# Second unit's rows ahead of weight words, weight words later, and own outputs in a bank of their own, in an mLSTM cell followed by a multiplicative FFN

## The chip, the cores and the metric

The kernel runs on one core of one Trainium2 chip. The metric is device time in microseconds (us), the median of several executions. A core has five engines with a queue each, and the text calls them as the profile does: PE is TensorE (PEld its weight loads), DVE is VectorE, ACT is ScalarE, POOL is GpSimd, SP is SyncE, which here only issues DMAs.

## The reference

```python
B, H, S, D = 4, 8, 768, 40                   # float32 throughout
for t in range(S):                           # mLSTM cell, per batch and head
    m_new  = maximum(f_gate[t] + m, i_gate[t])
    f_stab = exp(f_gate[t] + m - m_new);  i_stab = exp(i_gate[t] - m_new);  m = m_new
    C = f_stab * C + i_stab * outer(v[t], k[t])
    n = f_stab * n + i_stab * k[t]
    y[t] = sigmoid(o_gate[t]) * (C @ q[t]) / maximum(abs(n . q[t]), 1)
x = y as (3072, 320)                         # token rows, heads side by side
out = ((x @ w1) * (x @ w2)) @ w3 @ w_out     # w1, w2: 320 x 1024; w3: 1024 x 1024; w_out: 1024 x 320
```

## The kernel before

**Units and steps.** The recurrence is computed in chunks of 64 tokens; two chunks of one batch (128 tokens, all 8 heads) make a unit. There are 24 units, in order of token block and then batch, so four units are one block of 128 tokens of all batches, and a state is handed on every fourth unit. The main loop (line 727) has 32 steps. Step s loads the rows of unit s + 2 (`load`, `load_o`), computes scores, own weights and state of unit s, the outputs of unit s - 1, transposes k and q of unit s + 1 (`turn`), and makes the decay weights of unit s + 1 (`weights` on ACT, eight exponentials; `masks` on POOL). For the first four units the rows of those weights are spread over the partitions by matmuls (`spread`, tile `ub`), later they come from `UT` by a DVE transpose (`rows_of_u`) or by DMA (`load_u`).

**A unit on PE** (`quarter_work`, line 330) is four groups of small matmuls into the PSUM tiles `cell0` and `cell1`: `ph`, the outputs from the unit's own tokens (`pw` times v); `pi`, the outputs from the state; `ss`, the scores; `pc`, the sums for the state, from the v weighted on POOL (`weighted`, tile `vw`). Each group goes through the four 64 x 64 quarters of the array in turn (`quarters`). A quarter that crosses the halves puts the result of one half of the tokens on the other half of the partitions, so DVE adds `ph` to `h` in four parts (line 400).

**DVE after a unit** (`outputs` and the end of `quarter_work`): `h` from `pi` and the gate (line 395), the four adds, the scores' product (line 373), the state's second part (378 or 380), three passes for the denominator (408, 410, 411), the state's last part (386), then the sigmoid with the denominator and y (416, 418). The state's decay on POOL (line 327) waits for the second part, and the next masks stand behind it on POOL.

**FFN.** x is y transposed (`x_trans` on PE, tile `px`, copied by ACT to `xT`). `up` computes blocks of x w1 and x w2 into PSUM (`pa`, `pb`), `up_rest` adds the last 64 of the 320 rows (weights `wr`), ACT copies the one and DVE multiplies by the other. Up-projections start in step 4 (lists `n_up`, `ups`): steps 4 to 6 use the first half of the 1024 columns, step 7 is the first that uses the second half. w3 and w_out are folded into one matrix (`fold`), so `ffn_out` gives the output directly.

**Weight words.** w1, w2, w3 and w_out are read as 64-bit words and turned into float32 on the chip: `fetch` loads a tile of words by SP, `scale` is two ACT passes (lines 181 and 185; in the opening the second one runs on DVE), `to_f32` is two DVE passes (189 and 190). The tiles are, in order: five for the first half of w1, w2 and their last rows (numbers 0 to 4), five for the second half (5 to 9), eight of w_out, sixteen of w3. `n_cvt[s]` tiles are converted at the end of step s, after the exponentials and `out_gate` in ACT's order, and words are fetched up to a few tiles ahead of the conversions. There are four `raw` buffers and two more in idle memory at the start.

**Order.** PE's order is that of the program. From the opening on, the other engines' orders are held too (`keep_order`), the SP queue among them: a DMA that waits for a buffer holds up all DMAs behind it. `mps` hands out four PSUM banks in rotation to all that isn't `cell`.

Of the kernel before, what the change touches and what calls it, by code (L numbers as in the profile page):

```python
# [8 lines left out]
FP = mybir.dt.float32  # L9
U32 = mybir.dt.uint32  # L10
AF = mybir.ActivationFunctionType
OP = mybir.AluOpType
# [4 lines left out]
def kernel(  # L17
# [26 lines left out]
    nc = tc.nc  # L44
# [3 lines left out]
    P = 128  # L48
# [50 lines left out]
    quarters = ((0, 0), (1, 1), (0, 1), (1, 0))  # L99


    NB, NBQ = 4, 3
    N_DVE = N_U = 10
    q_all = const.tile([P, NBQ * H * DP], FP, name="q_all")
    qbuf = [q_all[:, i * H * DP:(i + 1) * H * DP].rearrange("p (h d) -> p h d", d=DP) for i in range(NBQ)]
    kbuf = [const.tile([P, H, DP], FP, name=f"kbuf{i}") for i in range(NB)]
    vbuf = [const.tile([P, H, D1], FP, name=f"vbuf{i}") for i in range(NB)]
    ident = const.tile([P, P], FP, name="ident")
    state = [[const.tile([P, NP, D1], FP, name=f"state{b}_{i}") for i in range(3)] for b in range(B)]
    aT = const.tile([P, NT2, BH], FP, name="aT")  # L110
    gT = const.tile([P, NT2, BH], FP, name="gT")
    wT = const.tile([P, NT2, BH], FP, name="wT")
    decay = const.tile([P, B * NP, NT], FP, name="decay")
    UT = const.tile([P, 2, NT2, BH], FP, name="UT")
    U_d = dram.tile([NT, BH, L], FP, name="U_d")
    NY = 15
    KC = KF + 1
# [6 lines left out]
        return src[b, :, c * P:(c + 1) * P, :].rearrange("h p d -> p h d")  # L124

    def load(n, which=slice(0, 3)):
        for dst, src in ((kbuf[n % NB][:, :, 0:D], k), (qbuf[n % NBQ][:, :, 0:D], q), (vbuf[n % NB][:, :, 0:D], v))[which]:
            if src is not q or n < N_DVE:
                nc.sync.dma_start(out=dst, in_=rows(src, n))  # L129

# [8 lines left out]
                                      in_=of.rearrange("p (r f) d -> r p (f d)", f=4))  # L139

    def load_o(n):
        o_t[n] = io.tile([P, H, D], FP, name="o_in", tag="o_in", bufs=4)
        nc.sync.dma_start(out=o_t[n], in_=rows(o_gate, n))

    def load_u(n):
# [127 lines left out]
    def cols_of_u():  # L273
        pu = mps([P, 2, GC // 2, GR, BH], "pu")
        for x in range(2):
            for e in range(2):
                for t in range(2):
                    for c in range(GC // 2):
                        t0 = c * P + x * L + t * 32
                        mm(pu[x * L + e * 32:x * L + (e + 1) * 32, t, c].rearrange("p g r -> p (g r)"),  # L280
                           U[:, t0:t0 + 32], ident[0:RG, 0:RG])
        for t in range(2):
            nc.scalar.copy(out=UT[:, t].rearrange("p (g c) r -> p c g r", g=GR), in_=pu[:, t])

    def rows_of_u(n):
        c, b = divmod(n, B)
# [32 lines left out]
    def weighted(n):  # L319
        c, b = divmod(n, B)  # L320
        vw_t[n] = sb.tile([P, H, D1], FP, name="vw", tag="vw")
        nc.gpsimd.tensor_tensor(out=vw_t[n], in0=vbuf[n % NB], op=OP.mult,
                                in1=wT[:, c, b * H:(b + 1) * H].unsqueeze(2).to_broadcast([P, H, D1]))

    def decayed(new, old, n, x):
# [4 lines left out]
    def quarter_work(s, rest):  # L330


        rest()

        def part(j, c0, n):
            return cell[j][:, :, c0:c0 + NP * n].rearrange("p x (n d) -> p x n d", d=n)

        ss, pc, pi = part(0, 0, L), part(0, NP * L, D1), part(1, 0, D1)
        ph = [cell[1][:, x, NP * D1:2 * NP * D1].rearrange("p (h d) -> p h d", d=D1) for x in range(2)]
        n = s - 1  # L340
        if 0 <= n < NU:
            pw, vt, qT = u_t.pop(n), vbuf[n % NB], qT_t.pop(n)
            before = before_t.pop(n)

            for hd in range(H // 2):
                for x, e in quarters:
                    hq = hd if x == e else hd + H // 2
                    mm(ph[x][halves[e], hd, :], pw[halves[x], hq, :], vt[halves[x], hq, :])
            for p in range(NP):
                for hip, x in quarters:  # L350
                    mm(pi[halves[x], hip, p, :], qT[heads[hip], p, halves[x]], before[x][heads[hip], p, :])
        n, first_read = s, None
        if n < NU:
            c, b = divmod(n, B)
            kt, vw = kbuf[n % NB], vw_t.pop(n)
            ends = range(2 if c < NT2 - 1 else 1)
            first, second, after = state[b]
            before_t[n] = first, second
            state[b] = after, second, first
            kT, qT, pw = kT_t.pop(n), qT_t[n], u_t[n]  # L360
            for p in range(NP):
                for hip, x in quarters:
                    mm(ss[halves[x], hip, p, :], kT[heads[hip], p, halves[x]], qT[heads[hip], p, halves[x]])
            for p in range(NP):
                for x, e in quarters:
                    if x in ends:
                        mm(pc[halves[e], x, p, :], kt[halves[x], 2 * p + e, :], vw[halves[x], 2 * p + e, :])
        den = None
        if 0 <= s - 1 < NU:
            den = outputs(s - 1, pi, ph)  # L370
        if n < NU:
            pv = pw.rearrange("p (n two) t -> p two n t", two=2)
            first_read = nc.vector.tensor_tensor(out=pv, in0=ss, in1=pv, op=OP.mult)
        with tc.issue_after(first_read.ins) if first_read else nullcontext():
            if n < NU:

                if c:
                    nc.vector.tensor_tensor(out=second, in0=pc[:, 0], in1=second, op=OP.add)
                else:
                    nc.vector.tensor_copy(out=second, in_=pc[:, 0])  # L380
                if len(ends) > 1:
                    decayed(after, second, n, 1)
            if den:
                done = den()
            if n < NU and len(ends) > 1:
                nc.vector.tensor_tensor(out=after, in0=pc[:, 1], in1=after, op=OP.add)
            if den:
                done = done()
        return done if den else first_read

    def outputs(n, pi, ph):
        c, b = divmod(n, B)
        hs = slice(b * H, (b + 1) * H)
        h = sb.tile([P, H, D1], FP, name="h", tag="h")
        nc.vector.tensor_tensor(out=h.rearrange("p (n two) d -> p two n d", two=2), in0=pi,
                                in1=gT[:, c, hs].rearrange("p (n two) -> p two n", two=2).unsqueeze(3)
                                .to_broadcast([P, 2, NP, D1]), op=OP.mult)
        for x, e in quarters:
            part = h[halves[x], 0:H // 2] if x == e else h[halves[x], H // 2:H]
            nc.vector.tensor_tensor(out=part, in0=ph[x][halves[e]], in1=part, op=OP.add)  # L400

        den = sb.tile([P, H, 1], FP, name="den", tag="den")

        def first():
            V = nc.vector
            V.tensor_scalar(out=den.bitcast(U32), in0=h[:, :, D:D1].bitcast(U32), scalar1=0x7FFFFFFF, scalar2=None,  # L408
                            op0=OP.bitwise_and)
            V.tensor_scalar(out=den, in0=den, scalar1=1.0, scalar2=2.0, op0=OP.max, op1=OP.mult)  # L410
            V.reciprocal(out=den, in_=den)
            return then

        def then():
            e = o_t.pop(n)
            nc.vector.scalar_tensor_tensor(out=e, in0=e, scalar=1.0, in1=den.to_broadcast([P, H, D]), op0=OP.add, op1=OP.mult)
            y_t[n] = sb.tile([P, DM + REM], FP, name="y", tag="y")
            return nc.vector.tensor_tensor(out=y_t[n][:, 0:DM].rearrange("p (h d) -> p h d", d=D), in0=h[:, :, 0:D],
                                           in1=e, op=OP.mult)

        return first

    def send(n):

# [59 lines left out]
    fetch("w12", 0, 0)  # L484
    load(0, slice(2, 3))
    fetch("w12", 1, 0)
    load_o(0)
    fetch("w12", 2, 0)
    idle += [w3o_words[:, i * CW:(i + 1) * CW] for i in range(2)]
    fetch("w12", 3, 0)  # L490
    fetch("w12", 4, 0)
    load(1)
    load_o(1)

    nc.vector.memset(on, 1.0)
    nc.vector.memset(on.rearrange("p (c t) -> p c t", t=L)[:, :, 0:1], 0.0)
# [2 lines left out]
    for i in range(NB):  # L499
        nc.gpsimd.memset(kbuf[i][:, :, D:DP], 0.0)  # L500
        if i < NBQ:
            nc.gpsimd.memset(qbuf[i][:, :, D:DP], 0.0)
        nc.gpsimd.memset(vbuf[i][:, :, D:D1], 1.0)
    for t in state:
        nc.gpsimd.memset(t[0], 0.0)
# [67 lines left out]
    nc.scalar.activation(out=g, in_=U, func=AF.Exp)  # L573
    scale_next(True)
    convert()
    scale_next(True)

    ffn = ctx.enter_context(tc.tile_pool(name="ffn", bufs=2))

# [138 lines left out]
    n_seven = [0] * 19 + [1] * 12 + [0]  # L718
    n_down = [0] * 17 + [2] * 6 + [1] * 7 + [0, 5]
    w12 = [("w12", i, part) for part in range(2) for i in range(2 * KF + 1)]  # L720
    todo = w12[KF * 2 + 1:] + [("wo", i, 0) for i in range(FO)] + [("w3", ko, part) for ko in range(FO) for part in range(2)]
    n_cvt = [2, 1, 1, 1, 2, 2, 3, 3, 3] + [2] * 7
    pinned, ahead = 32, 9
    behind = ExitStack()
    turned, converted, fetched = 0, 2, 2 * KF + 1

    for s in range(len(n_up)):
        if N_U <= s + 3 < NU:
# [84 lines left out]
                scale_next()  # L813
        if N_DVE <= s + 2 < NU:
            load_turned(s + 2)
        while todo and fetched < converted + (2 if s < 2 else 3 if s < ahead - 1 else 4):
            fetch(*todo.pop(0))
            fetched += 1
        if s + 1 == pinned:
# [32 lines left out]
```

## Time and profile before

| | |
|---|---|
| median of 6 runs | 452.76 us (449.69 to 455.21) |
| profiled execution | 452.9 us, span 451.0 |
| PE busy | 428.1 us (95%), 5303 matmul records |
| PE weight loads | 339.8 us (75%) |
| DVE busy | 308.8 us (68%) |
| ACT busy | 150.9 us (33%) |
| POOL busy | 82.0 us (18%) |
| DMA | 51.15 MB, mean 113 GB/s |
| PE busy by stage: 0 to 11, to 22, to 34, to 45, to 56 us | 5.1, 5.1, 12.0, 7.9, 8.6 us |
| PE busy from 150 to 400 us | 250.0 us |

The span is the time from the first to the last instruction; the device time holds 1.9 us more. Busy times overlap between engines. A float32 matmul is two records. Where the page shows a granted clock of 0.5, matmuls take twice as long; before the first change of the clock, at some 39 us, the records show 1.00 whatever the clock was. Of steps 0 to 3 little is dense work; from step 4 on up-projections fill PE.

### The profile page before, as it was taken

What the parts mean: (1) busy time and instruction counts of PE and PEld (TensorE: products, weight loads), DVE (VectorE), ACT (ScalarE), POOL (GpSimd) and SP (SyncE); (2) the same over time, 40 slices, a digit from 0 to 9 for tenths busy, and PEclk for the clock granted to TensorE, in tenths of its full rate; (3) what the DMA queues carried; (4) which work ended last, traced back from release to release, by engine and by line L of the source; (5) the groups of instructions that cost most, each with busy time, mean ns of one, the idle gap of its engine ahead of it and who ended that gap; (6) DMA issues with size and microseconds to landing.
All of it is one profiled execution on the core that took longest, in us unless ns stands there. A gap on an engine that the chain in (4) does not pass through costs nothing.

```text
span 451.0 us, 12926 instructions
## 1 busy us (share of the span) xinstructions
PE 428.1 (95%) x5303; PEld 339.8 (75%) x5303; DVE 308.8 (68%) x645; ACT 150.9 (33%) x409; POOL 82.0 (18%) x154
## 2 busy tenths in 40 slices
PE   4497799999999999999999999999999999999997
PEld 3396687888777888878777878778788777777774
DVE  6347768877958866976695959677698776445800
ACT  4345555666643552453033312203121111001110
POOL 3222534332302202220222203102020000000000
PEclk9998599999999999999999999999999999999999
DMA  8999917679889895779544584663211120000001
GB/s 206 176 181 213 132 32 139 124 161 183 220 175 195 175 189 157 149 160 164 111 86 122 115 158 107 137 122 97 58 32 37 36 49 16 15 16 15 1 30 44
DMA packets 135595, 51.15 MB, mean 113 GB/s; under 512 B 109744, under 2 KB 127344, under 8 KB 135536
## 3 DMA queue, kind: packets, MB, share of 16 engines
q1 hardware_dynamic: 131936, 46.29, 51.7%
q10 hardware_dynamic: 3600, 4.03, 2.6%
q8 instruction: 41, 0.67, 0.6%
q14 instruction: 18, 0.15, 0.1%
HBM read 44.50 MB, written 5.80 MB: 112 GB/s over the span
## 4 chain that ended last, share of the span: by engine, by line
PE 88%; DMA 3%; DVE 2%; SPq 2%; ACT 2%; issue 1%; POOL 1%; POOLq 0%; DVEq 0%; ACTq 0%
PE cell L92 23%; PE pa L92 22%; PE pb L92 14%; PE po L92 13%; PE wp L92 7%; PE p L92 5%; DMA q_all<-in_q_dram 2%; PE pt L95 2%; SPq L174 1%; PE px L95 1%; PE pu L92 1%; PE ub L92 1%; DMA raw<-in_moe_w_dram 1%; DVE h L400 1%; SPq L129 0%
## 5 line engine op out<-in xcount | busy, mean ns | idle before, releaser
L92 PE MATMUL pa<-xT,w 128*128 128x256 f32 x240 | 62.4, 392 | 2.5 <-ACT xT L458 2.5
L92 PE MATMUL po<-w3o,ab 128*128 128x320 f32 x224 | 61.8, 433 | 0.0
L92 PEld LDWEIGHTS po<-w3o,ab 128*128 128x128 f32 x224 | 42.4, 190 | 17.3 <-issue 0.4
L92 PEld LDWEIGHTS pa<-xT,w 128*128 128x128 f32 x240 | 45.6, 195 | 11.0 <-ACT xT L458 3.6
L327 POOL TENSOR_TENSOR state<-state,decay 128x164 f32<-128x164 f32 x40 | 20.4, 511 | 170.4 <-DVE den L408 168.5
L300 POOL TENSOR_SCALAR_AFFINE_SELECT pw<-pw 64x512 f32<-64x512 f32 x48 | 33.7, 703 | 68.6 <-ACT pw L295 67.0
L92 PE MATMUL pb<-xT,w 128*128 128x256 f32 x192 | 46.1, 384 | 0.0
L92 PE MATMUL cell<-w3o,ab 128*128 128x320 f32 x160 | 44.0, 432 | 0.0
L295 ACT ACTIVATE pw<-pw,aT 128x64 f32<-128x64 f32 x160 | 40.3, 339 | 2.8 <-ACT o_sb L706 2.8
L92 PEld LDWEIGHTS pb<-xT,w 128*128 128x128 f32 x192 | 37.2, 194 | 5.3
L604 DVE TENSOR_TENSOR ab<-pb,a_sb 128x512 f32<-128x512 f32 x24 | 16.5, 690 | 34.4 <-ACT a_sb L603 34.4
L92 PEld LDWEIGHTS cell<-w3o,ab 128*128 128x128 f32 x160 | 30.4, 190 | 12.0
L651 DVE SCALAR_TENSOR_TENSOR a_sb<-pa,wo 128x512 f32<-128x512 f32 x12 | 8.3, 692 | 41.8 <-PE pa L92 41.8
L603 ACT ACTIVATE a_sb<-pa 128x512 f32<-128x512 f32 x24 | 14.3, 597 | 67.3 <-PE pb L92 67.3
L92 PE MATMUL pa<-xT,wr 64*64 64x256 f32 x384 | 36.8, 386 | 0.0
L92 PE MATMUL pb<-xT,wr 64*64 64x256 f32 x384 | 36.2, 379 | 0.0
L92 PE MATMUL wp<-wo,w3T 128*128 128x320 f32 x128 | 35.8, 432 | 0.0
L400 DVE TENSOR_TENSOR h<-cell,h 64x164 f32<-64x164 f32 x96 | 31.3, 326 | 1.8
L92 PEld LDWEIGHTS wp<-wo,w3T 128*128 128x128 f32 x128 | 23.7, 190 | 8.9
L92 PEld LDWEIGHTS pa<-xT,wr 64*64 64x64 f32 x384 | 19.0, 132 | 14.8 <-issue 8.9
L706 ACT COPY o_sb<-po 128x320 f32<-128x320 f32 x14 | 6.0, 427 | 67.4 <-PE po L92 67.4
L92 PEld LDWEIGHTS pb<-xT,wr 64*64 64x64 f32 x384 | 20.2, 133 | 3.0
(132 smaller groups left out, 735.4 us busy)
## 6 DMA issues: line engine op xcount, KB each, us to landing
raw<-in_moe_w_dram SPq DMA_DIRECT2D x64, 128.0 KB, 3.3
kbuf<-in_k_dram SPq DMA_DIRECT2D x24, 160.0 KB, 4.5
vbuf<-in_v_dram SPq DMA_DIRECT2D x24, 160.0 KB, 5.1
o_in<-in_o_gate_dram SPq DMA_DIRECT2D x24, 160.0 KB, 4.4
out_dram<-o_sb ACTq DMA_DIRECT2D x24, 160.0 KB, 1.8
raw<-in_moe_w_dram SPq DMA_DIRECT2D x7, 512.0 KB, 5.9
pw<-U_d SPq DMA_DIRECT2D x28, 128.0 KB, 4.0
raw<-in_moe_w_out_dram SPq DMA_DIRECT2D x32, 80.0 KB, 2.1
```

The costliest lines, as they stand in the source:

```text
L92: in_order(nc.tensor.matmul(out, lhsT=lhsT, rhs=rhs, start=start, stop=stop))
L95: in_order(nc.tensor.transpose(out, in_, ident[0:n, 0:n]))
L174: nc.sync.dma_start(out=dst, in_=src)
L295: nc.scalar.activation(out=pw[:, h, :], in_=src[:, h, :], func=AF.Exp, bias=aT[:, c, b * H + h:b * H + h + 1])
L300: nc.gpsimd.affine_select(out=pw[r], in_=pw[r], compare_op=OP.is_ge, fill=0.0, base=0, pattern=[[0, H], [1, L]], channel_multiplier=-1)
L327: nc.gpsimd.tensor_tensor(out=new, in0=old, op=OP.mult, in1=decay[:, b * NP:(b + 1) * NP, 2 * c + x:2 * c + x + 1] .to_broadcast([P, NP, D1]))
L400: nc.vector.tensor_tensor(out=part, in0=ph[x][halves[e]], in1=part, op=OP.add)
L603: nc.scalar.mul(out=a_sb, in_=pa, mul=UP ** -2)
L604: nc.vector.tensor_tensor(out=ab_t[gr][j][:, fs[0]:fs[-1] + 1, t0:t0 + a_sb.shape[-1]], in0=pb, in1=a_sb, op=OP.mult)
L651: nc.vector.scalar_tensor_tensor(out=out, in0=p, scalar=UP ** -2, in1=q, op0=OP.mult, op1=OP.add)
L706: nc.scalar.copy(out=o_sb, in_=po)
```

## The change

Four edits that belong together:

1. **Order of the first loads.** k and q of unit 1 are loaded right behind the second word tile, its v and o next, and the third word tile after them. Tiles 3 and 4 are no longer fetched in the opening. How many tiles are fetched by the end of steps 0 to 7 is now given by a list (`n_fetch`), and conversions (`n_cvt`) come later: by the end of steps 0 to 8 there were 4, 5, 6, 7, 9, 11, 14, 17, 20 tiles converted, now 2, 3, 4, 5, 6, 8, 12, 16, 20. One scaling in the opening is left out with them.
2. **Own outputs of the first five units.** `ph` of units 0 to 4 gets one of the rotating banks, each head's result on its own tokens' partitions, with two quarters of the array in place of four; DVE adds it in one instruction of full size.
3. **The denominator's passes.** The first now stands ahead of the scores' product, the second behind it, the third behind the state's second part.
4. **Buffers.** v and o have five buffers in place of four. `UT` keeps four token blocks in place of six, and its copy is narrower.

```diff
-    NB, NBQ = 4, 3
+    NB, NBQ, NBV = 4, 3, 5
     N_DVE = N_U = 10
+    N_DIAG = 5
...
-    vbuf = [const.tile([P, H, D1], FP, name=f"vbuf{i}") for i in range(NB)]
+    vbuf = [const.tile([P, H, D1], FP, name=f"vbuf{i}") for i in range(NBV)]
...
-    UT = const.tile([P, 2, NT2, BH], FP, name="UT")
+    GC = NT // 3
+    UT = const.tile([P, 2, GC, BH], FP, name="UT")
...
-        o_t[n] = io.tile([P, H, D], FP, name="o_in", tag="o_in", bufs=4)
+        o_t[n] = io.tile([P, H, D], FP, name="o_in", tag="o_in", bufs=5)
...
-            nc.scalar.copy(out=UT[:, t].rearrange("p (g c) r -> p c g r", g=GR), in_=pu[:, t])
+            nc.scalar.copy(out=UT[:, t].rearrange("p (g c) r -> p c g r", g=2), in_=pu[:, t, :, 0:2])
...
-            for hd in range(H // 2):
+            if n < N_DIAG:
+                ph = mps([P, H, D1], "ph")
+                for hq in range(H):
+                    for r in halves:
+                        mm(ph[r, hq, :], pw[r, hq, :], vt[r, hq, :])
+            for hd in range(H // 2 if n >= N_DIAG else 0):
                 for x, e in quarters:
...
             den = outputs(s - 1, pi, ph)
+            den()
         if n < NU:
             pv = pw.rearrange("p (n two) t -> p two n t", two=2)
             first_read = nc.vector.tensor_tensor(out=pv, in0=ss, in1=pv, op=OP.mult)
         with tc.issue_after(first_read.ins) if first_read else nullcontext():
+            if den:
+                den()
...
             if den:
-                done = den()
+                den()
             if n < NU and len(ends) > 1:
                 nc.vector.tensor_tensor(out=after, in0=pc[:, 1], in1=after, op=OP.add)
             if den:
-                done = done()
+                done = den()
...
-        for x, e in quarters:
+        if n < N_DIAG:
+            nc.vector.tensor_tensor(out=h, in0=ph, in1=h, op=OP.add)
+        for x, e in quarters if n >= N_DIAG else ():
...
-        def first():
+        def steps():
             V = nc.vector
-            V.tensor_scalar(...0x7FFFFFFF...)
+            yield V.tensor_scalar(...0x7FFFFFFF...)
-            V.tensor_scalar(out=den, in0=den, scalar1=1.0, scalar2=2.0, op0=OP.max, op1=OP.mult)
-            V.reciprocal(out=den, in_=den)
-            return then
+            yield V.tensor_scalar(out=den, in0=den, scalar1=1.0, scalar2=2.0, op0=OP.max, op1=OP.mult)
+            yield V.reciprocal(out=den, in_=den)
...
     fetch("w12", 1, 0)
+    load(1, slice(0, 2))
     load_o(0)
+    load(1, slice(2, 3))
+    load_o(1)
     fetch("w12", 2, 0)
     idle += [w3o_words[:, i * CW:(i + 1) * CW] for i in range(2)]
-    fetch("w12", 3, 0)
-    fetch("w12", 4, 0)
-    load(1)
-    load_o(1)
...
     scale_next(True)
     convert()
-    scale_next(True)
...
-    todo = w12[KF * 2 + 1:] + [("wo", i, 0) ...
+    todo = w12[3:] + [("wo", i, 0) ...
-    n_cvt = [2, 1, 1, 1, 2, 2, 3, 3, 3] + [2] * 7
+    n_cvt = [0, 1, 1, 1, 1, 2, 4, 4, 4] + [2] * 7
+    n_fetch = [4, 5, 6, 8, 10, 12, 16, 20]
...
-    turned, converted, fetched = 0, 2, 2 * KF + 1
+    turned, converted, fetched = 0, 2, 3
...
-        while todo and fetched < converted + (2 if s < 2 else 3 if s < ahead - 1 else 4):
+        while todo and fetched < (n_fetch[s] if s < len(n_fetch) else converted + 4):
```

More of the change, by code (lines that the diff above doesn't have):

```diff
@@ L126, in load @@
     def load(n, which=slice(0, 3)):
-        for dst, src in ((kbuf[n % NB][:, :, 0:D], k), (qbuf[n % NBQ][:, :, 0:D], q), (vbuf[n % NB][:, :, 0:D], v))[which]:
+        for dst, src in ((kbuf[n % NB][:, :, 0:D], k), (qbuf[n % NBQ][:, :, 0:D], q), (vbuf[n % NBV][:, :, 0:D], v))[which]:
             if src is not q or n < N_DVE:
@@ L321, in weighted @@
         vw_t[n] = sb.tile([P, H, D1], FP, name="vw", tag="vw")
-        nc.gpsimd.tensor_tensor(out=vw_t[n], in0=vbuf[n % NB], op=OP.mult,
+        nc.gpsimd.tensor_tensor(out=vw_t[n], in0=vbuf[n % NBV], op=OP.mult,
                                 in1=wT[:, c, b * H:(b + 1) * H].unsqueeze(2).to_broadcast([P, H, D1]))
@@ L341, in quarter_work @@
         if 0 <= n < NU:
-            pw, vt, qT = u_t.pop(n), vbuf[n % NB], qT_t.pop(n)
+            pw, vt, qT = u_t.pop(n), vbuf[n % NBV], qT_t.pop(n)
             before = before_t.pop(n)
-            for hd in range(H // 2):
+            if n < N_DIAG:
[4 more added lines that the diff above has]
+            for hd in range(H // 2 if n >= N_DIAG else 0):
                 for x, e in quarters:
@@ L404, in outputs @@
         den = sb.tile([P, H, 1], FP, name="den", tag="den")
-        def first():
+        def steps():
             V = nc.vector
-            V.tensor_scalar(out=den.bitcast(U32), in0=h[:, :, D:D1].bitcast(U32), scalar1=0x7FFFFFFF, scalar2=None,
+            yield V.tensor_scalar(out=den.bitcast(U32), in0=h[:, :, D:D1].bitcast(U32), scalar1=0x7FFFFFFF, scalar2=None,
                             op0=OP.bitwise_and)
-            V.tensor_scalar(out=den, in0=den, scalar1=1.0, scalar2=2.0, op0=OP.max, op1=OP.mult)
-            V.reciprocal(out=den, in_=den)
-            return then
-        def then():
+            yield V.tensor_scalar(out=den, in0=den, scalar1=1.0, scalar2=2.0, op0=OP.max, op1=OP.mult)
+            yield V.reciprocal(out=den, in_=den)
             e = o_t.pop(n)
@@ L417, in then @@
             y_t[n] = sb.tile([P, DM + REM], FP, name="y", tag="y")
-            return nc.vector.tensor_tensor(out=y_t[n][:, 0:DM].rearrange("p (h d) -> p h d", d=D), in0=h[:, :, 0:D],
+            yield nc.vector.tensor_tensor(out=y_t[n][:, 0:DM].rearrange("p (h d) -> p h d", d=D), in0=h[:, :, 0:D],
                                            in1=e, op=OP.mult)
-        return first
+        done = steps()
+        return lambda: next(done)
     def send(n):
@@ L502 @@
             nc.gpsimd.memset(qbuf[i][:, :, D:DP], 0.0)
+    for i in range(NBV):
         nc.gpsimd.memset(vbuf[i][:, :, D:D1], 1.0)
@@ L720 @@
     w12 = [("w12", i, part) for part in range(2) for i in range(2 * KF + 1)]
-    todo = w12[KF * 2 + 1:] + [("wo", i, 0) for i in range(FO)] + [("w3", ko, part) for ko in range(FO) for part in range(2)]
-    n_cvt = [2, 1, 1, 1, 2, 2, 3, 3, 3] + [2] * 7
+    todo = w12[3:] + [("wo", i, 0) for i in range(FO)] + [("w3", ko, part) for ko in range(FO) for part in range(2)]
+    n_cvt = [0, 1, 1, 1, 1, 2, 4, 4, 4] + [2] * 7
+    n_fetch = [4, 5, 6, 8, 10, 12, 16, 20]
     pinned, ahead = 32, 9
     behind = ExitStack()
-    turned, converted, fetched = 0, 2, 2 * KF + 1
+    turned, converted, fetched = 0, 2, 3
     for s in range(len(n_up)):
```

## The prediction

> **What bounds the kernel now.** I read the page's strip of 40 slices first, then what TensorE waited for, then its timeline, and last the other engines' timelines around two places.
>
> ```profile
> span 451.0 us, 12926 instructions
> ...
> PE   4497799999999999999999999999999999999997
> ...
> PEclk9998599999999999999999999999999999999999
> ```
>
> From the sixth slice on TensorE is full: 428.1 us busy of 451.0, and of the 22.9 idle only 2.3 lie between 57 us and 400 us (0.84 at 69.9, 0.31 at 106.3, 1.11 at 126.4). So the first 57 us can give something back, and after them every new wait of TensorE is paid in full. Its waits, as total, times and longest:
>
> ```profile
> PE pt L95 <- DMA kbuf<-in_k_dram: 10.3, 2, 5.7
> PE cell L92 <- POOL vw L322: 3.8, 3, 2.6
> PE pa L92 <- ACT xT L458: 2.5, 3, 1.1
> PE pt L95 <- DMA q_all<-in_q_dram: 0.9, 1, 0.9
> ```
>
> The 10.3 us are two waits: 5.7 for the very first rows, which the change leaves, and the second unit's. The timeline shows that one (start, duration, and in brackets the idle time and what ended it), and the first up-projection of two later steps:
>
> ```profile
> 19.32 1.09 PE L95 MATMUL pt<-ident,kbuf 128*128 128x128 f32 x4 [4.60 <-DMA kbuf<-in_k_dram]
> 21.26 1.09 PE L95 MATMUL pt<-ident,q_all 128*128 128x128 f32 x4 [0.85 <-DMA q_all<-in_q_dram]
> ...
> 51.75 3.78 PE L92 MATMUL pa<-xT,w 128*128 128x256 f32 x8 [0.57 <-ACT xT L458]
> ...
> 82.79 1.89 PE L92 MATMUL pa<-xT,w 128*128 128x256 f32 x8
> 84.52 1.67 PE L92 MATMUL pb<-xT,w 128*128 128x256 f32 x7
> ```
>
> The 3.78 at 51.75 against 1.89 for the same eight matmuls is the clock: it was granted at half there.
>
> **Rows of the second unit ahead: -5.6 us at 22 us.** The SyncE queue issues k(1) at 9.85 and q(1) at 10.64, behind five word tiles; they are in use at 19.32 and 21.26. In the new order they follow the second word tile, whose issue ended at 5.22, so they are issued at about 5.3 and 5.7. Issue to landing is 5.7 (k, median of the first 60 us; 9.3 at most) and 6.1 (q; 10.5 at most): landed at 11 to 12, at the very worst 16.2. TensorE's work before them ends at 14.71 and q is wanted 0.9 later. Both waits go. Eight such transposes took 1.95 in step 1 (31.13 to 33.08), so the spreading of step 0 starts at 14.71 + 1.95 = 16.7, not at 22.27: 5.6 earlier. Bounds: 5.0 with the worst landing of q, 5.6.
> What is late next is a chain of computation: from the spreading in step 1 to the up-projection at 51.75 it runs TensorE (spread), ScalarE (eight exponentials, 1.75), GpSimd (two masks 1.38, weighting 0.74 to 0.79), TensorE, transposes, and round again, some 9 us a step. Nothing in the change touches it, so the gain is carried to step 4. The third early scaling that goes from the opening frees ScalarE 0.7 and VectorE 0.43 beside a TensorE that does not wait for them: 0. The narrower copies of line 283 (0.54 for two) save a third at most, behind the exponentials: 0.
> The word tiles that come later are used later too: tile 4 (numbered from 0) is converted at the end of step 3, and by the rows of that step is ready 4.7 us after 51.75 (56.48), wanted 6.2 after it (57.96) at half clock: 0. At full clock it would be wanted 3.5 after: +1.2, but then 2.5 of half clock are saved.
>
> **Five units' own outputs in one bank: +0.9 +0.9 on TensorE.** As many matmuls (32 records a unit), but in two quarters of the array in place of four in turn. Four quarters took 0.43 per unit at full clock (58.81 to 59.24), 0.88 at half (27.54 to 28.42). The nearest row with two column halves is the spreading: 32 in 1.98 (62 ns each) against 0.88 (27 ns) at half clock, so I take double. From below it is 0, if issue and not the array sets the pace. Step 1: +0.9 on the path. Steps 2 and 3: TensorE waits 2.6 and 0.7 for GpSimd's weighting after these, so 0 (at most 0.9 if the slack of step 3 goes). Steps 4 and 5, where TensorE is full: 2 x 0.43 = +0.9. VectorE saves three of four adds (1.34 for four; one of full size like line 395, 0.49): 0.85 a unit, five times. No wait of TensorE is on it, since weighting on GpSimd ends the wait in steps 2 and 3: 0. The extra turn in the four rotating banks is read out in time by the rows of steps 4 and 5: 0. The spreading of step 2 ran at 1.15, as the clock had just risen; 5.6 earlier it may still be slow: +0.4, from 0 to 0.8.
>
> **Denominators' passes spread: 0.** The second pass takes 0.46 on 8 columns where the first takes 0.16: 0.3 is waiting for the first, and goes, per unit. One pass now stands ahead of the scores' product (0.2 later). VectorE idles in the full stage, so neither is paid.
>
> **Five buffers of v and o: 0.** They free the SyncE queue from line 129's wait for TensorE (0.2) and line 143's; no TensorE wait after 22 us names a load of rows.
>
> **Conversions later: +3.4 us in step 7.** Counting the list: before, 11 tiles are converted by the end of step 5; after, 8, and step 6 does tiles 8 to 11. Step 7 is the first that reads the second half of the words, tiles 5 to 9, and tile 8 (w2, second row block) is the second operand of the first pb. It stands in ScalarE's queue behind the exponentials and the gate of step 6, and VectorE waits for ScalarE:
>
> ```profile
> 83.56 2.02 ACT L295 ACTIVATE pw<-pw,aT 128x64 f32<-128x64 f32 x8
> 85.48 0.47 ACT L261 ACTIVATE o_in<-o_in 128x320 f32<-128x320 f32 x1
> ...
> 65.12 0.68 ACT L181 ACTIVATE raw<-raw 128x512 f32<-128x512 f32 x1
> ...
> 65.83 0.77 DVE L189 TENSOR_SCALAR w<-raw 128x512 uint32<-128x512 uint32 x1 [0.18 <-ACT raw L181]
> 66.73 1.00 DVE L190 CUSTOM_DVE_ANT_0 w<-raw,w 128x1024 uint16<-128x1024 uint16 x1
> ```
>
> The scaling can start at 85.84 (where the first of step 6 starts now). A tile of this size took 65.12 to 67.73 = 2.6 from its scaling to its end, so it is ready at 88.4. pb starts at 84.52 and does its first block (two records of 0.22) by 85.0. TensorE stands for 3.4 us. Behind the waiting matmul the whole step is queued: rest, cell, transposes. With GpSimd silent the second pass would end 0.69 (as at 29.36) after the scaling, which takes 1.25 (65.12 to 66.37): ready at 87.8, a wait of 2.8. Tile 9 follows by 1.2 and is wanted 5 later: 0. One wo tile more in each of steps 6 to 8 (0.8 ScalarE, 0.85 to 1.1 VectorE) fits their idle time (2.66 and 1.65 at 88 to 91), except in step 8, where VectorE ends at 116.39 just as its next operand is there: up to 0.9 later into the chain that ends in the 1.11 wait; I take +0.3.
>
> **The clock after that wait: +1.7.** The rows of 2 us (columns: span, busy time and count of TensorE, its weight loads, VectorE, ScalarE, GpSimd, then clock, DMA share, GB/s):
>
> ```profile
> 36.00:38.00 2.00, 0.00 (x0) 0.00 (x0) 0.97 (x2) 1.42 (x3) 1.82 (x3) 1.00 1.32 138
> ...
> 40.00:42.00 2.00, 2.00 (x18) 1.67 (x18) 1.92 (x6) 1.60 (x3) 0.35 (x1) 0.50 0.87 242
> ```
>
> After 2.6 idle (35.7 to 38.3) the clock fell to half for about 3.4 us, though TensorE was busy by then. Idle times of 1.11 and 0.84 did nothing. So 3.4 us of idle should cost half of 3.4 = 1.7; bounds 0 and 5 (below).
> The Trainium skill (TensorE: Matmul & The Clock Gate, section HAM oscillation — how this bites in real kernels) has as its abstract rule that gaps over about 3.4 us are to be avoided. Taken as a threshold, it leaves this one at the edge; with no fall the sum would be 453.2 in place of 454.9. The row at 36 speaks against so high a threshold.
>
> **Sum,** from the profiled execution's 452.9 (451.0 span, 1.9 around it): -5.6 +0.9 +0.4 +0.9 +3.4 +0.3 +1.7 = 454.9. That execution lies 0.1 above the median 452.76, so 454.8 as a median.
>
> **Rivals.**
> *No stall in step 7* (the tile is there after all): 454.9 - 3.4 - 1.7 = 449.8; with a luckier clock in the opening (the half clock at 51.75 cost about 2.7) down to 447. For it: VectorE and ScalarE have idle time in step 6. Against: that time comes before the exponentials' data. 0.15.
> *Stall, clock unmoved*: 453.2; 451 if the opening also warms earlier. 0.23.
> *Slower: the clock stays low after the stall.* From 47 to 57 it was at half for 10 us, since short waits kept coming. If step 7 is followed by the same, the loss is 5.0 and not 1.7: 458.2. It decides if the half clock lasts over 8 us there. Against: what follows the stall is dense. 0.12.
> *The rows do not come earlier* (the queue full, as the third word tile's 2.31 issue hints): the gain is about 2.6, 457.9. 0.03.
>
> **Numbers.** Forecast 454.8 with 0.47, its own range 453.5 to 457.5. Range 449.6 to 458.4: it leaves out the lower half of the first rival and the end of the slow ones. Within 1% is 448.2 to 457.3, about what a measurement of this kernel can tell from no change. Faster by over 1%: a part of the first rival and unseen gains, 0.10. Slower: the two slow rivals and the forecast's tail, 0.23. Same: 0.67.
>
> **What would show it.** No wait before the transposes of unit 1; step 4's first up-projection at 47 to 49 us; own-output matmuls of the first five units at 0.9 us; a TensorE wait of about 3 us on the conversion (line 190) in front of pb near 82 us, and a granted clock of half behind it. The prediction is wrong if the steps 1 to 3 do not keep their 9 us, or if that wait is missing.

## The result and the profile after

The changed kernel takes 454.36 us (median of 37 runs; the kernel before, in its runs beside it, 451.32 of 74): a ratio of 1.0081, 95% interval 1.0063 to 1.0099. The ratio is taken from runs in the faster of two states, so it is not the quotient of the two medians (1.0067). It is 0.8% slower, where 0.45% was forecast. The sum came out close, but two of its terms were far off, in opposite directions.

The page's head and strips of the changed kernel (the profiled execution took 456.5 us):

```profile
span 454.7 us, 12899 instructions
...
PE   4987998899779999999999999999999999999997
...
PEclk9976899999969999999999999999999999999999
```

TensorE is busier than before in slices 2 and 5, but has a new hole in slices 7 and 8 (at about 80 us) and another in slices 11 and 12 (at about 125 us), with a second stretch of reduced clock in slice 12. What TensorE waited for, as total, times, longest:

```profile
PE pa L92 <- ACT xT L468: 7.3, 3, 5.9
PE pt L95 <- DMA kbuf<-in_k_dram: 5.6, 1, 5.6
PE cell L92 <- POOL vw L324: 4.9, 4, 2.2
PE pb L92 <- DVE w L192: 3.5, 1, 3.5
```

The 10.3 us for rows of k are down to 5.6: the second unit's wait is gone. The 3.5 in front of pb is the wait that was forecast; the 5.9 for xT was 1.1 before. TensorE's timeline of the changed kernel at the places the prediction speaks of:

```profile
14.48 1.06 PE L95 MATMUL pt<-ident,kbuf 128*128 128x128 f32 x4
...
16.32 1.98 PE L92 MATMUL ub<-gates,ident 96*64 96x64 f32 x32
18.23 1.93 PE L92 MATMUL pu<-ident,gates 96*32 96x96 f32 x32
...
43.29 3.78 PE L92 MATMUL pa<-xT,w 128*128 128x256 f32 x8 [0.57 <-ACT xT L468]
...
75.52 1.89 PE L92 MATMUL pa<-xT,w 128*128 128x256 f32 x8
77.25 0.59 PE L92 MATMUL pb<-xT,w 128*128 128x256 f32 x2
81.30 1.56 PE L92 MATMUL pb<-xT,w 128*128 128x256 f32 x6 [3.46 <-DVE w L192]
...
128.12 3.78 PE L92 MATMUL pa<-xT,w 128*128 128x256 f32 x8 [5.85 <-ACT xT L468]
```

The same matmuls in the kernel before, where the prediction does not show them:

```profile
22.27 1.98 PE L92 MATMUL ub<-gates,ident 96*64 96x64 f32 x32
24.18 3.43 PE L92 MATMUL pu<-ident,gates 96*32 96x96 f32 x32
...
127.47 1.99 PE L92 MATMUL pa<-xT,w 128*128 128x256 f32 x8 [1.11 <-ACT xT L458]
```

Read as a balance of the two profiled executions (1.6 and 2.2 us above their medians): the spreading of step 0 starts 5.95 us earlier than before (16.32 against 22.27), step 4's first up-projection 8.46 earlier (43.29 against 51.75), step 7 7.27 earlier (75.52 against 82.79). Behind the 3.46 us wait, step 8 has 3.6 left (its up-projection starts at 91.23 against 94.78). At 128.12 the lead is a lag of 0.65 (against 127.47), and the up-projection there runs at half clock, 3.78 for eight matmuls; that makes the lag about 3.7, the difference of the spans.

The first wait is tile 8, as forecast: ScalarE reaches its scaling behind the exponentials, and VectorE ends its second pass at 81.24.

```profile
78.56 0.66 ACT L183 ACTIVATE raw<-raw 128x512 f32<-128x512 f32 x1
...
80.25 0.99 DVE L192 CUSTOM_DVE_ANT_0 w<-raw,w 128x1024 uint16<-128x1024 uint16 x1
```

The second is longer to follow. ScalarE's timeline of the changed kernel shows the copy of xT for unit 7 (line 468) behind the scalings of tiles 20 to 23, each of which waits for its own words:

```profile
119.51 0.69 ACT L183 ACTIVATE raw<-raw 128x512 f32<-128x512 f32 x1 [4.42 <-DMA raw<-in_moe_w_dram]
...
122.10 0.70 ACT L183 ACTIVATE raw<-raw 128x512 f32<-128x512 f32 x1 [1.34 <-DMA raw<-in_moe_w_dram]
...
124.35 0.67 ACT L183 ACTIVATE raw<-raw 128x512 f32<-128x512 f32 x1 [1.00 <-DMA raw<-in_moe_w_dram]
...
126.52 0.65 ACT L183 ACTIVATE raw<-raw 128x512 f32<-128x512 f32 x1 [0.95 <-DMA raw<-in_moe_w_dram]
...
127.61 0.46 ACT L468 COPY xT<-px 128x384 f32<-128x384 f32 x1
```

Why the words are late stands in the SP queue's timeline of the changed kernel. It does nothing from 75.89 on, until at 81.27 the conversion of tile 8 frees a buffer; from there to 122.44 it issues 67 DMAs, 0.61 us each, with hardly a gap, and tiles 20 to 23 are the last sixteen:

```profile
74.86 1.03 SPq L145 DMA_DIRECT2D o_in<-in_o_gate_dram  x1
81.27 8.41 SPq L176 DMA_DIRECT2D raw<-in_moe_w_out_dram  x16
...
113.95 8.49 SPq L176 DMA_DIRECT2D raw<-in_moe_w_dram  x16
```

In the kernel before the last sixteen end at 121.76, 0.7 us earlier than here, though its step 7 begins 7.3 us later:

```profile
113.09 8.67 SPq L174 DMA_DIRECT2D raw<-in_moe_w_dram  x16
```

While the queue stands, the DMA engines stand too (mean busy share 0.00 from 78 to 82 us). From 82 to 94 us their share is 0.5 to 0.6 while the queue issues nearly all the time, so there they are not what limits; where it is near 1.0 (94 to 100, 106 to 112 and from 118 us on) they may have a part, which no run separates.

**Theory A** after this reading: the order of the first loads brings the opening's gain; the later conversions take it back twice, once directly (tile 8) and once through the SP queue, whose four fetches per step each wait for a conversion of the same step, and which is then too full to get step 9's words there in time. **Rivals:** the words come no later than before, and the second wait is only TensorE's earlier arrival; the opening's gain comes from the lighter opening and not from the order; the second wait is one of DMA bandwidth or of ScalarE's load, and has nothing to do with the first; the own bank or the freed buffers matter more than costed.

### The profile page after: what moved, and what is told of

It reads as the page before. It is cut to its first block, busy times and chain, and to the rows that moved or that the text cites. A ratio compares the mean times of both kernels' runs of the same rounds, so it can differ in the third digit from the quotient of the medians.

```text
span 454.7 us, 12899 instructions
## 1 busy us (share of the span) xinstructions
PE 430.0 (95%) x5303; PEld 341.5 (75%) x5303; DVE 299.9 (66%) x629; ACT 151.0 (33%) x410; POOL 81.5 (18%) x155
## 4 chain that ended last, share of the span: by engine, by line
PE 85%; DVE 4%; issue 4%; DMA 2%; ACT 2%; POOL 2%; SPq 0%; DVEq 0%; POOLq 0%; ACTq 0%
PE cell L92 22%; PE pa L92 22%; PE pb L92 14%; PE po L92 13%; PE wp L92 7%; PE p L92 5%; DMA raw<-in_moe_w_dram 2%; PE pt L95 1%; PE px L95 1%; POOL pw L302 1%; DVE pw L381 1%; DVE h L412 1%; ACT pw L297 1%; POOL vw L324 1%; PE ub L92 0%
## 5 line engine op out<-in xcount | busy, mean ns | idle before, releaser
L92 PE MATMUL pa<-xT,w 128*128 128x256 f32 x240 | 64.1, 400 | 7.3 <-ACT xT L468 7.3
L92 PEld LDWEIGHTS pa<-xT,w 128*128 128x128 f32 x240 | 46.7, 199 | 16.1 <-ACT xT L468 8.3
L92 PE MATMUL pb<-xT,w 128*128 128x256 f32 x192 | 47.9, 394 | 3.5 <-DVE w L192 3.5
L92 PEld LDWEIGHTS pb<-xT,w 128*128 128x128 f32 x192 | 38.3, 200 | 9.7 <-DVE w L192 3.9
L412 DVE TENSOR_TENSOR h<-cell,h 64x164 f32<-64x164 f32 x76 | 24.8, 326 | 1.4
L183 ACT ACTIVATE raw<-raw 128x512 f32<-128x512 f32 (+1 forms) x32 | 20.2, 630 | 7.7 <-DMA raw<-in_moe_w_dram 7.7
```

The lines of the kernel that those rows point to most:

```text
L92: in_order(nc.tensor.matmul(out, lhsT=lhsT, rhs=rhs, start=start, stop=stop))
L183: nc.scalar.activation(out=hi, in_=hi, func=AF.Prelu, scale=2.0 ** -111, alpha=2.0 ** 32)
```

## The experiments

Ratios are to the kernel before in runs on the same chip, with 95% intervals; the changed kernel has 1.0081 (1.0063 to 1.0099).

**Order of the first loads alone, on the kernel before** (`rows_only`).

```diff
     fetch("w12", 1, 0)
+    load(1, slice(0, 2))
     load_o(0)
+    load(1, slice(2, 3))
+    load_o(1)
     fetch("w12", 2, 0)
...
     fetch("w12", 4, 0)
-    load(1)
-    load_o(1)
```

> The kernel before with one edit: k, q, v and o of unit 1 loaded behind the second word tile, in front of the third; its conversions and fetches as they were. Theory A (the opening gains, the later words lose): the first up-projection of step 4, at 51.8 us before and 43.3 after the change, comes at 43 to 45; no wait on a conversion in step 7; the SP queue keeps its distance to step 7, so the wait before the 126 us up-projection stays near 1 us. Time 8 us under the kernel before, 1.5 to 2% faster. Rival B (the opening's 8.5 us are owed to the lighter opening, fewer word tiles fetched and converted in it): step 4 starts at 47 or later, gain of 4 us at most.

Measured: 0.9924 (0.9887 to 0.9962). No wait in step 7, none over 1 us later; but step 4 starts at 50.77 only. Both numbers, a gain of 0.8% (3.4 us) and a step 4 later than 47, are those of rival B; but the reason is another, which ScalarE's and TensorE's timelines of this kernel show:

```profile
12.70 0.71 ACT L181 ACTIVATE raw<-raw 128x512 f32<-128x512 f32 x1
20.96 0.69 ACT L181 ACTIVATE raw<-raw 128x512 f32<-128x512 f32 x1 [7.56 <-DMA raw<-in_moe_w_dram]
21.54 0.38 ACT L553 COPY gT<-pg 128x96 f32<-128x96 f32 x2
21.79 0.62 ACT L317 COPY kT<-pt 128x512 f32<-128x512 f32 x1
```
```profile
21.97 3.43 PE L92 MATMUL pu<-ident,gates 96*32 96x96 f32 x32 [3.62 <-ACT gT L553]
```

The third early scaling now waits 7.56 us for a tile that comes behind the rows, and every copy that unit 1 needs stands behind it on ScalarE. The one deleted line `scale_next(True)` in the change is thus a condition of its early step 4.

**The same without that scaling** (`rows_light`; `- scale_next(True)` behind the second `convert()` of the opening, as in the change).

> rows_only without the third early scaling of the opening. In rows_only ScalarE stood 7.6 us for the third word tile, with the copies of gT, kT(1) and qT(1) behind that scaling. Theory A (that scaling has to go with the order of the loads, and is what the opening's gain hangs on): the matmuls of cols_of_u follow the spreading of step 0 with no wait (18.4 in place of 22.0), the first up-projection of step 4 at 42 to 46 according to the clock, 4 to 6 us under rows_only. Rival B (fewer conversions in steps 0 to 2 make the opening quick): step 4 starts at 49 or later.

```profile
18.52 1.93 PE L92 MATMUL pu<-ident,gates 96*32 96x96 f32 x32
...
46.39 1.99 PE L92 MATMUL pa<-xT,w 128*128 128x256 f32 x8 [0.57 <-ACT xT L458]
...
74.94 1.89 PE L92 MATMUL pa<-xT,w 128*128 128x256 f32 x8
...
119.71 1.99 PE L92 MATMUL pa<-xT,w 128*128 128x256 f32 x8 [1.36 <-ACT xT L458]
```

TensorE's timeline: the wait in front of `pu` is gone, step 4 starts at 46.4, and does so at full clock (1.99). Theory A's place is right. The 3.1 us to the changed kernel's 43.3 are not separated: here TensorE waits 0.9 and 0.3 us for the rows of unit 2, which stand behind five word tiles, and the clock is at half from 25 to 46 us. By step 7 the lead is 7.85 us (74.94), more than the changed kernel's 7.27, and with the old conversions the wait at xT stays at 1.36, no clock falls behind it, and the lead is kept (spans 443.3 and 451.0). So TensorE's earlier arrival alone does not make the second wait. In time the gain over the first of the two kernels is not resolved: 0.9924 (0.9886 to 0.9962), medians 446.8 and 448.6 us in the two batches, where 4 to 6 us less was expected. Still, order and scaling alone, with the old conversions, make a kernel faster than the one before.

**Tile 8 converted one step earlier, in the changed kernel** (`tile8_early`).

```diff
-    n_cvt = [0, 1, 1, 1, 1, 2, 4, 4, 4] + [2] * 7
-    n_fetch = [4, 5, 6, 8, 10, 12, 16, 20]
+    n_cvt = [0, 1, 1, 1, 1, 3, 3, 4, 4] + [2] * 7
+    n_fetch = [4, 5, 6, 8, 10, 13, 16, 20]
```

> The changed kernel with tile 8 converted one step earlier: three conversions in step 5 and three in step 6 in place of two and four, one fetch more by the end of step 5. Both theories: the 3.46 us wait in front of pb in step 7 goes. Theory A (the SP queue is full from step 6's conversions on, and sets when the words of step 9 are there): only 4 of the 51 DMAs in front of these words are out of the way, about 2 us at 0.5 each; the wait for xT near 122 us grows from 5.9 to about 7, and the time falls by about 2 us. Rival B (the two waits are independent): the time falls by 3.5 us.

Measured: 1.0017 (0.9982 to 1.0052), 0.6% or 2.9 us under the changed kernel, between the two expectations and no help in choosing. The waits decide: that in front of pb is gone, and of its 3.46 us 1.6 come back at xT:

```profile
124.81 3.54 PE L92 MATMUL pa<-xT,w 128*128 128x256 f32 x8 [7.46 <-ACT xT L468]
```

So the two waits hang together, as theory A has it; the second one differs by 1.2 us between profiles of the changed kernel itself (5.85, and 4.62 below).

**Conversions 2, 3, 3, 3 in steps 4 to 7, in the changed kernel** (`words_early`; `n_cvt = [0, 1, 1, 1, 2, 3, 3, 3, 4] + [2] * 7`, `n_fetch` as in the last).

> The changed kernel with conversions of 2, 3, 3, 3 in steps 4 to 7 in place of 1, 2, 4, 4 (tiles 8 and 9 done in step 5) and fetches to match, so that no fetch of step 6 waits for a tile of the first half's tail. Theory A: the 3.46 us wait goes, the SP queue gets to the words of step 9 some 5 to 7 us earlier, the wait for xT near 122 us falls to 2 to 4 us, time 6 to 9 us under the changed kernel (9 if the half clock behind that wait goes with it). Rival B (step 9's words are late for another reason, such as DMA bandwidth): 3.5 us and the wait of 5.9 us stays.

Measured: 0.9856 (0.9804 to 0.9908), 2.2% or some 10 us under the changed kernel by the ratios, 8.2 us by the medians (446.18 against 454.36), and faster than the kernel before. The wait for xT is down to 3.56, with the half clock still behind it:

```profile
117.12 3.78 PE L92 MATMUL pa<-xT,w 128*128 128x256 f32 x8 [3.56 <-ACT xT L468]
```

In this profile step 4 starts at 39.0, 4.3 us ahead of the changed kernel's, with the matmuls at the full rate from 18 us on (the spreadings of steps 1 and 2 take 1.15 us each; in the changed kernel 1.15 and 1.98). The edit does not touch steps 0 to 3, so how much of the gain is the opening's is not known.

Five of the kernels give the rule of the second wait (us; each number from TensorE's or the SP queue's rows):

| kernel | from step 7's first pa to the last issue of tiles 20 to 23 | last issue to the waiting pa | wait |
|---|---|---|---|
| before | 39.0 | 5.7 | 1.1 |
| order alone, without the scaling | 39.1 | 5.6 | 1.4 |
| changed | 46.9 | 5.7 | 5.9 |
| tile 8 earlier | 44.8 | 5.9 | 7.5 |
| 2, 3, 3, 3 | 41.4 | 5.5 | 3.6 |

The pa starts 5.5 to 5.9 behind the last issue in all five, whatever the wait: the SP queue sets it. With the old conversions the queue needs 39 us from step 7 on, with the change's 47. The wait is what is left after TensorE's own time to there, 43.2 to 43.6 (46.8 with the first wait in it).

**ScalarE's queue: the scalings of tiles 22 and 23 behind the copy of xT, in the changed kernel** (`xT_first`; `pinned, ahead = 32, 10` in place of 9).

> The changed kernel with one number altered (ahead 10 in place of 9): scalings two tiles ahead of their conversion begin in step 10, not in step 9, so that ScalarE copies xT of unit 7 behind the scalings of tiles 20 and 21 and not behind those of 22 and 23 too. Theory A (the 5.9 us wait at 122 us is ScalarE's queue standing for words that the SP queue issued late, and the half clock from 128 to 134 us is that wait's): xT is copied at about 123.4 in place of 127.6, the wait falls to 1.5 to 2 us, the clock stays up (3.2 us more): 4 to 7.5 us under the changed kernel. Rival B (the words are late and only the place of the wait changes): the wait comes back in step 10 or 11 at the conversions of tiles 22 and 23, less than 2 us gained.

Measured: 1.0010 (0.9976 to 1.0045), 0.7% or 3.2 us under the changed kernel. TensorE's timeline:

```profile
77.78 2.50 PE L92 MATMUL pb<-xT,w 128*128 128x256 f32 x6 [3.45 <-DVE w L192]
...
120.39 1.95 PE L92 MATMUL pa<-xT,w 128*128 128x256 f32 x8
...
137.97 1.99 PE L92 MATMUL pa<-xT,w 128*128 128x256 f32 x8 [1.93 <-ACT xT L468]
```

The 5.85 are gone altogether and the clock stays up at 120; 1.93 come back one step on, at the next copy of xT, so rival B has a part. The gain is under theory A's range, and the first row gives one reason: in this profile the clock did fall behind the first wait (2.50 for six matmuls that took 1.56 in the changed kernel).

**Both: 2, 3, 3, 3 and `ahead` 10** (`words_early_xT`, the best kernel).

> words_early with the same number altered (ahead 10). Theory A: the 3.6 us wait for xT falls to 0 to 1 us and the half clock behind it goes; 3 to 6 us under words_early, 2 to 2.5% under the kernel before. Rival B: within 1 us of words_early.

Measured: 0.9795 (0.9749 to 0.9841): 2.05% faster than the kernel before, some 2.8% faster than the change. It is the best of all kernels run, and beats both given ones. What TensorE waited for in it:

```profile
PE pt L95 <- DMA kbuf<-in_k_dram: 5.5, 1, 5.5
PE cell L92 <- POOL vw L324: 3.4, 4, 2.1
PE pa L92 <- ACT xT L468: 1.6, 3, 0.8
PE pa L92 <- DVE wr L192: 1.1, 1, 1.1
```

Both new waits are gone. The step from 2, 3, 3, 3 alone is 0.6%, 2.7 us, a little under the 3 to 6 expected, and the intervals overlap.

**Own outputs in four quarters again, in the changed kernel** (`four_quarters`; `N_DIAG = 0`).

> The changed kernel with the own outputs of all units in four quarters and four adds again (N_DIAG 0). Theory A (the bank of its own costs 0.4 us on TensorE in steps 1, 4 and 5 and gives VectorE time that nothing waits for): 0.8 to 1.2 us faster than the changed kernel, the matmuls of own outputs at 0.43 us in steps 4 and 5. Rival B (one add in place of four lets steps 1 to 3 turn round faster): slower by 1 to 3 us, the first up-projection of step 4 later than 43.3 us.

Measured: 1.0041 (0.9997 to 1.0084), 0.4% under the changed kernel with overlapping intervals, and a median of 455.63 us that is above its 454.36: not resolved. Step 4 starts at 45.41, later than 43.3 as rival B has it, but with the clock at half longer (`pu` took 3.43). In its profile the clock falls behind the first wait:

```profile
82.17 2.93 PE L92 MATMUL pb<-xT,w 128*128 128x256 f32 x6 [3.46 <-DVE w L192]
```

**The same in the best kernel** (`best_four`).

> words_early_xT with the own outputs of all units in four quarters and four adds again. With both waits gone TensorE is full from step 4 on. Theory A: 0.8 us less on TensorE in steps 4 and 5, 0 to 1 in the opening: 1 to 2 us faster than words_early_xT, if the clock goes the same way. Rival B (one add shortens the opening's turns): 1 to 4 us slower.

Measured: 0.9841 (0.9782 to 0.9900) against 0.9795 without it: no difference that these runs can tell, and the other sign. Step 4 starts at 39.55 there, so four quarters do not by themselves make the opening late. What the matmuls cost is settled by the rows: in the changed kernel `ph` of step 4 starts at 50.63 and the next group at 51.42 to 51.50, 0.8 us where four quarters took 0.43. That the whole edit gains or loses is not shown.

**Denominators and buffers undone, in the changed kernel** (`undo_rest`; passes together behind the scores' product; `NBV` 4, `o_in` with four buffers; the narrower `UT` stays).

> The changed kernel with the denominator's passes together again behind the scores' product and with four buffers of v and o in place of five. Theory A (nothing waits for either): same time as the changed kernel within 0.3%, the same waits of 3.5 us in step 7 and of 5 to 6 us near 122 us. Rival B (the freed SP queue and the shorter VectorE chain matter): 1 to 3 us slower.

Measured: 1.0064 (1.0032 to 1.0096), within 0.2% of the changed kernel, waits of 3.4 and 5.4 us at the same places. VectorE is busy 304.6 us in it and 299.9 in the changed kernel: 4.7 us less busy time that nothing waited for. Theory A holds.

**The changed kernel once more** (`after_again`), to see whether its profile is typical.

> The changed kernel itself, beside the others on one chip. Theory A: 0.6 to 1% over the kernel before; the wait of 3.4 to 3.5 us in front of pb in step 7 and a wait of 5 to 6 us for xT near 122 us again. Which stretches run at half clock may differ: behind the first wait (as in two of four profiles with that wait), in steps 2 to 4. Rival B (the profile first seen was unlike the others): the second wait is under 3 us or the clock alone makes the difference.

Measured: 1.0096 (1.0059 to 1.0133). Its waits:

```profile
PE pa L92 <- ACT xT L468: 6.0, 3, 4.6
...
PE pb L92 <- DVE w L192: 3.5, 1, 3.5
```

The first wait is the same; the second, 4.6, is a little under the 5 to 6 expected and far over rival B's 3.

**Tile 4 converted in step 2, in the best kernel** (`best_wr`).

> words_early_xT with tile 4 (wr) converted in step 2 and not in step 3: conversions 0, 1, 2, 1, 1 in steps 0 to 4, one fetch more by the end of step 2. In words_early_xT the clock is up by step 4 and TensorE waits 1.1 us for this tile in front of the last rows of the first up-projection. Theory A: that wait goes, 1 us faster. Rival B (VectorE's queue in step 3 holds up outputs that steps 3 and 4 need): the 1.1 us come back in front of the transposes px or pa, no gain or a loss of 1 us.

Measured: 0.9890 (0.9831 to 0.9948), 1% slower than without, with intervals that just overlap. The wait for wr is gone, but in its profile TensorE stands still within the scores of step 3, for nothing that the profile names:

```profile
41.57 0.62 PE L92 MATMUL cell<-qT,kT 40*64 40x64 f32 x26 [2.80 <-issue]
```

The first 6 of 32 scores are done at 38.8, the other 26 wait. The kernel before stands 1.6 us at the same instruction, 2, 3, 3, 3 and the best with four quarters 0.6 to 0.7, the changed kernel not at all. It may be this stand or the clock of the opening (`pu` took 3.43 in this profile) that costs the 1%; the conversion is not shown to. What holds TensorE there stays open.

## Why the prediction was right, and where it was not

**Rows ahead, -5.6: right** (measured -5.95, 16.32 against 22.27). The third scaling was costed at 0 as "beside a TensorE that does not wait for them"; that holds with the scaling gone, but kept it costs 3.6 us in front of `pu`, as the first experiment shows.

**"+0.4" for the clock of the opening: wrong in sign and size.** The prediction let one spreading run slow (the one at 33.01, which is step 1's and not step 2's), because the clock had risen only at 33 us before; it took 1.15 us as before. With the hole of 4.6 us closed it rose at about 18: `pu` took 1.93 in place of 3.43, and from the spreading of step 0 to that of step 1 went 7.7 us in place of 10.7; the next two stretches took 8.9 and 10.4, where 8.5 and 10.3 were. So the 9 us a step were not kept in step 1, and step 4's first up-projection came at 43.3, not at 47 to 49. The gain at step 4 is 8.46 where 5.6 - 0.9 - 0.4 = 4.3 was carried there. That the shorter idle time is the cause is argued from the rows, and it is not enough by itself: `pu` took 1.93 to 2.08 in nine of the eleven profiles without hole and without third scaling, and 3.43 in two. Step 4 started at 39.0 to 46.4 in the profiles of kernels with rows ahead and no third scaling, so this term varies by itself by some 7 us.

**Own outputs, +0.9 on TensorE in steps 4 and 5: right in size,** 0.8 us a unit where 0.43 was; its worth in the whole is not resolved.

**Denominators and buffers, 0 and 0: right** (undone, 0.2%).

**Tile 8 in front of pb, +3.4: right** (3.39 to 3.46 in the five profiles of kernels with the change's lists).

**The clock behind it, +1.7: not so in the changed kernel.** In both its profiles, and with denominators and buffers undone, pb and pa behind the wait run at full clock; in those with `ahead` 10 and with four quarters they do not: half clock in two of five. An idle time of 3.4 us is at the edge here: the row of 36 to 38 us before, where 2.6 sufficed, was no safe threshold. Behind the longer second waits (4.62, 5.44 and 5.85 us in the first three of these profiles) the clock did fall each time. The Trainium skill (TensorE: Matmul & The Clock Gate, section HAM oscillation — how this bites in real kernels) has the rule of no TensorE gaps over about 3.4 us. The waits of the full stage agree with it better than with the row I went by; in the opening the clock fell with shorter ones (2.6 us before, 2.16 us in the changed kernel).

**"Up to 0.9 later into the chain that ends in the 1.11 wait; I take +0.3": the step that failed.** It counted one more conversion on VectorE, and found idle time for it. It did not follow the fetches: four per step, each behind a conversion of the same step, on a queue that holds all later loads. The wait grew by 4.7 us (1.11 to 5.85) where 0.3 was taken, and the half clock behind it took about 3 more: pa and pb from 128.12 to 134.86, 6.7 us for what took 3.7 before.

So the sum came out by luck, by two errors that cancel: some 4 us more gain in the opening, and some 7.5 us more loss at 122 to 135, less 1.7 that did not occur: 454.9 + 7.4 - 4.2 - 1.7 = 456.4, against 456.5 in the profiled execution. The range held; the reasoning held for the rows of the second unit, for the own outputs in steps 4 and 5, and for the first wait.

## What to carry to other kernels

When work is moved later in a kernel whose loads go through one ordered queue, follow the loads that wait for the work's buffers, and then count what stands behind them in the queue: here the queue stood 5.4 us at 76 us, reached the words of step 9 some 8 us later after step 7 than before, and TensorE waited 4.7 us longer at 122. See that a tile converted at the end of a step is not wanted at the start of the next (tile 8, converted in step 6, cost step 7 3.46 us; converted in step 5, nothing), and put copies that the critical engine waits for ahead of work that itself waits for a load on the same engine. An order of loads and the order of the work on them belong together: one scaling left in its old place took back 4.4 of the 5.4 us that step 4 began earlier, though the two kernels' times do not differ beyond the noise.

## What the runs showed of the hardware

Idle time of one length was followed by half clock in some profiles and not in others. In the opening, a wait of 2.15 or 2.16 us for the weighted v came with half clock in the changed kernel and not in 2, 3, 3, 3; one of 2.61 us did so before (at 36 us) and not in the best kernel with four quarters (at 27 us). In the full stage, from step 4 on, 0.84 to 1.93 us never did, 3.39 to 3.46 us did in two of five profiles, and 3.56 and the longer ones (4.62 to 7.46) always did. The start of step 4 differed by several us between profiles of nearly the same code, as the clock of the opening did (43.3 and 43.4 in two of the changed kernel, 39.0 to 45.4 in close relatives), which is as much as most of the edits here are worth.
